# Sliding-window attention regrouped: 32-query groups, shared columns for half-used key blocks, and 128x64 matmul tiles

## The chip, the cores and the metric

The kernel runs on one core of a Trainium2 chip. The metric is the device time of one execution in microseconds (us). Lower is better.

## The reference

Two kinds of layer alternate, twice each, on 2048 tokens of width 512 with 32 heads of 16. The first is linear attention, the second sliding attention in which a query sees itself and the 255 keys before it.

```python
def _A_ref(x, wqkv, wo):            # H = 32, Dh = 16
    q, k, v = ...                   # x @ wqkv, split into heads
    phi = lambda t: jnp.where(t > 0, t + 1, jnp.exp(t)) + 1e-6
    pq, pk = phi(q), phi(k)
    kv = jnp.einsum("bhsd,bhse->bhde", pk, v)
    z = jnp.einsum("bhsd->bhd", pk)
    num = jnp.einsum("bhqd,bhde->bhqe", pq, kv)
    den = jnp.einsum("bhqd,bhd->bhq", pq, z)[..., None] + 1e-6
    return ... (num / den) ... @ wo

def _B_ref(x, wqkv, wo):            # W = 256
    scores = jnp.einsum("bhqd,bhkd->bhqk", q, k) * (Dh ** -0.5)
    mask = (idx[:, None] - idx[None, :] >= 0) & (idx[:, None] - idx[None, :] < W)
    p = _softmax(jnp.where(mask[None, None], scores, -1e9), axis=-1)
    return ... jnp.einsum("bhqk,bhkd->bhqd", p, v) ... @ wo

x = A_x
x = x + _A_ref(_layernorm(x), A_wqkv, A_wo)
x = x + _B_ref(_layernorm(x), B_wqkv, B_wo)
x = x + _A_ref(_layernorm(x), A_wqkv, A_wo)
x = x + _B_ref(_layernorm(x), B_wqkv, B_wo)
```

## The kernel before

The tokens lie in 16 tiles of 128 rows (`xres`), and every stage is written per tile. Each stage is a list of operations, each of which names its engine, what it reads and writes, and a function that emits its instructions. The order of all operations is a table of numbers, `ORDER`; a number with `:a.b` also names the buffers it takes, and one with `'` takes its second engine. The kernel walks the table, takes buffers from rings, and puts a semaphore wait where a dependency needs it. So layers overlap freely: keys of the next linear layer are made while the sliding layer before it still runs.

PE is the matmul engine, ACT does exponentials and copies out of PSUM, DVE the other elementwise work, POOL the reciprocal roots of the layer norm (`rstd`) and the transfers that lay out value blocks, SP the queue of the transposing transfers. PSUM has eight banks, `ps`; one unit of scores takes two pairs of them.

**Linear layer.** `a_kv` normalizes a tile, makes keys (`pk`) and values (`vA`, 17 columns a head with a one for the sum). `kv_mm` multiplies them into sums for groups of eight heads: four 128x128 matmuls of 136 columns a tile. In the first layer these add up in one PSUM pair; in the second, groups of tiles are added by DVE into `kvacc`. `sums` masks off the blocks between different heads, `a_q` and `a_out` do the queries.

**Sliding layer.** `b_qkv` makes queries `qT`, keys `kbd` and values `vbd`. Heads come in pairs: a block of 64 keys of both heads fills the 128 columns of one weight tile, so that scores come out with 2 x 64 keys on the partitions and queries along the columns. `vbd` is the matching block layout of the values, written by four small transfers a tile on POOL. `b_attn` takes 128 queries. They see six 64-key blocks: four middle ones go with all 128 queries, of the oldest only the first 64 queries are needed and of the newest only the last 64. The eight head-pair columns are f (four) x r (four row tiles of 32 that run side by side in PE).

- `sH`: scores of the two half-used blocks, 32 matmuls of 64 columns. `eH0`, `eH1`: two exponentials of 1024 elements into `pH`. `mH0`, `mH1`: two masks of `pH` on DVE, with the triangles of `tri`.
- `s0` to `s3`: scores of the four middle blocks, one unit per f, 16 matmuls of 128 columns. `e00` to `e31`: two exponentials of 1024 elements per unit into `pF`. `m0` to `m3`: one mask of 512 elements per unit.
- `u0h`, `u1h`: products of `pH` with values, 16 matmuls of 34 columns each. A part of 64 queries is padded with zeros to 128 columns, which is what `pH`'s third of zeros is for. `u00` to `u11`: products of `pF`, 16 each.
- `dr`, `dm`: division on DVE. `wo`: output projection and residual.

Tiles 0 and 1 see fewer blocks; the very last tile is written by `b_end`, which masks with matmuls (L1072) instead of DVE.

In the profile: L1016 is `sH`, L1065 `s0` to `s3`, L1044 `eH`, L1086 `e..`, L1052 `mH`, L1104 `m..`, L1122 the products of `pH`, L1134 those of `pF`, L863 and L875 the projections, L921 `kv_mm`, L947 the products of the linear layer's queries, L850 copies out of PSUM, L884 and L887 the two exponential or relu steps of `phi`, L990 the value transfers, L822 `rstd`, L1328 the adds into `kvacc`.

Of the kernel before, what the change touches and what calls it, by code (L numbers as in the profile page):

```python
# [9 lines left out]
ALU = mybir.AluOpType  # L10
# [333 lines left out]
617:4.3 618 619:0 448:2 405 851:0.2.0 415 852 853 416 631 592 632 417:3 625:7.2.5 406 633:0 626 878:4.0.1 622:6.3 623 648 879 880 649 467:3.10.3 468 627' 854  # L344
620 624' 634:4 428:4.0 429 873 469 418:3 650 593 449:2 471 882:0.6.2 883 884 450 482:3.11.1 483 855:1 860:0 861 856 430 431 470 857 621 432:1 451 484 903
651:1 858:1 935:4.6.0 486 862 863:2 859:0 864 885 419:2 420 421 635:3.4 936 874:0.4.3 485 872 433:0 652:0 636 937 607:2.0.0 875 876 608 909:0.6.4 637':1 904
910 911 865:1 62 609' 640:3.0 641 666 653:2.5 638 913:0.4.5 628 654 914 915 643:7.1.1 644 877 886:6 639 667 881 642' 668 629 610 611 655':2 669:2 912 891:3
887 970:0.4.1 645 646 888 702 703 889:3 890:2 938 866:2 892 893 971 972 67 656 894:0 895 657 905:0.6.0 906 867 434:5 435 868 907 944:0.3.3 436 658:2.1 1391
945 908 946 458:6.1 659 459 684 460 472 661:5.2.2 662 670:1 461 660 685 1392 462:3 686 704 917:0.3.1 1393 663' 921:2 922 923 463:2 896:3 918 919 948:0.6.2
924:2 647 916 920 671:5.0 949 950 672 473:3.3 925:1 474 705:3 926:2 1394:0 1395:0 927 487 475 687:1 673:0 1005:0.6.2 1006 476 477:0 928 676:5.2 677 929:0 930  # L350
1007 940:0.3.0 941 464:2 465 897:7 951 942 678' 979:0.5.4 980 688:3 706:2 478:1 931:0 1008 939 466 898 674 1401:4.1 1402 899 981 943 947 952:0.2.5 953
# [4 lines left out]
712:3.0 715:2.2.0 716 1021 1420:1 738 1421:2 1001:1 739 713 1013 709':2 1430 710 1431 717' 1026:5 501 499 500 714' 1022:0.6.1 1023 1024 1409:4.5.2 1410  # L356
1396:2.7.3 1397 1411 1027 711 1025 1412 1053:0.6.2 1413 1422:3.2.1 1423 1432 1052 1398 1054 1055 1028 1424 1399 1400 1031:4 1032 1033 1029:2 1433:3 724:4
1030:1 1434:5 1425 1034:3 1110:0.6.2 1111 1112 725:2.3 726 1426 1035 1427:5.0 727':0 1045:0.3.0 1428 1046 758 718 1002:2 740 741:2 1078 742:0 1003 1047 1429'
1084:0.6.3 1004 1445 1446 683 1056 1414:5.5 730:4.1 1085 1044 1415 1057:0.2.5 1086 1058 728 1048 731 1416' 1440:7.2 1441 732 1059 759:1 1447 729 1435:6.0.2
1442' 1060 1436 1437 1088:0.4.1 1438 1439 1089 1087 502 1061:3 1062 1066:2 1090 1063 1036:0 1064:0 1079 1065:2 1145:0.6.0 1146 760:3 1067 748:5.2 1091 719  # L360
1068 701 1080:0.3.0 1069:1 1070 1147 1081 1082 749 503:6.2 1448:0 504 750' 733:2.1.5 734 743:5.4 735 505 506 1083 736 507:3 1119:0.3.4 1120 1121 744 745':1
1114 751:2.2.1 752 746 508:2 1071:3 747 753' 1149 1092:0.6.2 1093 1037:5 1038 1096:4 1097 1094 1095 1449:3 1039 1123:0.2.5 1124 1098 1125 1101:7 1102 1099:3
# [76 lines left out]
class _Kernel:  # L439
# [496 lines left out]
    def bmask(self, hf):  # L936
        return self.bm8.h[:].unsqueeze(1).unsqueeze(3).to_broadcast([P, 2, 8, 17])
# [443 lines left out]
```

## Time and profile before

| | us |
|---|---|
| median of 3 runs | 414.5 (414.13 to 414.88) |
| profiled execution | 414.87 |
| its span, first to last instruction | 413.6 |
| PE busy | 399.4 |
| ACT busy | 376.6 |
| DVE busy | 370.5 |
| POOL busy | 104.8 |

The granted clock of PE is 1.0 throughout. An engine's busy time counts an instruction from its start to its end; those of PE, and in part those of ACT and DVE, overlap with the next one, so that the time from start to start is the price of one in a row of them. The first layer's part runs from 0 to about 60 us, the linear layer in the middle from about 220 to 260; sliding attention fills the rest, mixed with the neighbouring linear layers.

### The profile page before, as it was taken

How to read it: one execution, taken by the hardware profiler on the slowest of the kernel's cores; microseconds unless marked ns; L12 is line 12 of the kernel's file. 1: busy time of each engine (PE TensorE's matmuls, PEld its weight loads, DVE VectorE, ACT ScalarE, POOL GpSimd, SP SyncE). 2: the span in 40 equal slices, each digit the busy share in tenths (PEclk: the TensorE clock that was granted, in tenths of full speed). 3: DMA queues.
4: the chain of work that ended last, by engine and by line, in shares of the span. 5: the costliest groups of instructions: out<-in, count | busy, mean ns of one | idle time of the engine just before them, and what ended most of it. 6: DMA issues, size and time to landing. Idle time of an engine off the chain costs nothing.

```text
span 413.6 us, 18932 instructions
## 1 busy us (share of the span) xinstructions
PE 399.4 (97%) x8394; PEld 284.3 (69%) x8394; DVE 370.5 (90%) x979; ACT 376.6 (91%) x485; POOL 104.8 (25%) x204
## 2 busy tenths in 40 slices
PE   7999999999999999999999999999999999999998
PEld 2654877776676767777686678676767776867765
DVE  6996799999999999999998999999999999887873
ACT  5998769999999999999999467899999999999996
POOL 2420025162053121411313000260533232311300
DMA  8539224526243235222122102331375453261433
GB/s 259 145 84 217 43 61 80 101 60 99 46 55 57 48 51 69 50 35 61 42 49 55 41 2 40 70 75 32 80 81 76 68 107 34 55 93 30 58 54 92
DMA packets 76808, 29.48 MB, mean 71 GB/s; under 512 B 66352, under 2 KB 74672, under 8 KB 76720
## 3 DMA queue, kind: packets, MB, share of 16 engines
q1 hardware_dynamic: 71424, 22.63, 29.7%
q0 software_dynamic: 4096, 4.46, 6.1%
q8 instruction: 68, 1.11, 1.2%
q10 hardware_dynamic: 1200, 1.11, 0.9%
q14 instruction: 20, 0.16, 0.2%
HBM read 6.29 MB, written 2.10 MB: 20 GB/s over the span
## 4 chain that ended last, share of the span: by engine, by line
PE 50%; ACT 34%; DVE 11%; DMA 3%; issue 1%; SPq 0%; DVEq 0%
ACT pF L1086 24%; PE ps L863 21%; PE ps L875 10%; ACT pH L1044 7%; PE ps L1134 6%; PE ps L1065 5%; PE ps L1122 3%; DVE o L959 2%; DMA w_Av<-in_A_wqkv_dram 2%; PE ps L1016 1%; DVE stats L819 1%; DMA oT<-o 1%; PE ps L921 1%; PE ps L947 1%; DVE pk L890 1%
## 5 line engine op out<-in xcount | busy, mean ns | idle before, releaser
L1086 ACT ACTIVATE pF<-ps 128x1024 bf16<-128x1024 f32 x240 | 229.6, 1083 | 4.4 <-PE ps L1065 2.6
L822 POOL TENSOR_TENSOR rstd<-mv,const 128x1 f32<-128x1 f32 x64 | 37.6, 594 | 211.9 <-DVE mv L820 194.2
L990 POOL DMA_DIRECT2D vbd<-vt x128 | 67.3, 533 | 73.8 <-DVE vt L850 48.6
L1134 PE MATMUL ps<-vbd,pF 128*128 128x34 bf16 x1856 | 62.2, 178 | 1.9 <-issue 1.9
L1044 ACT ACTIVATE pH<-ps 128x1024 bf16<-128x1024 f32 (+1 forms) x64 | 60.3, 1014 | 2.6 <-PE ps L1016 2.3
L1134 PEld LDWEIGHTS ps<-vbd,pF 128*128 128x128 bf16 x1856 | 54.7, 96 | 8.4 <-issue 2.1
L1104 DVE TENSOR_TENSOR pF<-pF,const 128x512 bf16<-128x512 bf16 (+2 forms) x116 | 47.1, 413 | 5.6 <-ACT pF L1086 5.2
L1065 PE MATMUL ps<-qT,kbd 32*128 32x128 bf16 x1920 | 48.7, 217 | 1.9 <-ACT pF L1086 0.6
L884 ACT ACTIVATE E<-ps 128x512 bf16<-128x512 f32 x64 | 38.6, 622 | 10.4 <-PE ps L875 7.8
L819 DVE BATCH_NORM_STATS2 stats<-xres 128x6 f32<-128x512 bf16 x64 | 43.4, 684 | 1.9 <-DMA xres<-in_A_x_dram 1.6
L1052 DVE TENSOR_TENSOR pH<-pH,const 128x1024 bf16<-128x1024 bf16 (+1 forms) x64 | 41.1, 644 | 0.4 <-ACT pH L1044 0.4
L1065 PEld LDWEIGHTS ps<-qT,kbd 32*128 32x128 bf16 x1920 | 28.2, 92 | 17.7 <-ACT pF L1086 7.0
L875 PE MATMUL ps<-xT,w_Bk 128*128 128x128 bf16 x512 | 35.5, 219 | 0.7 <-ACT xT L850 0.3
L875 PE MATMUL ps<-xT,w_Bq 128*128 128x128 bf16 x512 | 35.6, 219 | 0.2 <-ACT pF L1086 0.2
L1122 PEld LDWEIGHTS ps<-vbd,pH 128*128 128x128 bf16 x928 | 29.2, 96 | 9.4 <-issue 3.1
L863 PE MATMUL ps<-w_Av,xTa 128*128 128x512 bf16 (+2 forms) x134 | 33.9, 369 | 1.4 <-DMA w_Av<-in_A_wqkv_dram 1.2
L875 PE MATMUL ps<-xTa,w_Aq 128*128 128x128 bf16 x512 | 34.8, 219 | 0.2 <-DVE pq L888 0.2
L863 PE MATMUL ps<-w_Bv,xT 128*128 128x512 bf16 (+2 forms) x144 | 34.2, 356 | 0.6 <-ACT pF L1086 0.3
L863 PE MATMUL ps<-w_Bo,oT 128*128 128x512 bf16 (+2 forms) x141 | 34.5, 354 | 0.3
L1122 PE MATMUL ps<-vbd,pH 128*128 128x34 bf16 x928 | 32.8, 178 | 1.3 <-DVE pF L1104 0.5
L863 PE MATMUL ps<-w_Ao,oT 128*128 128x512 bf16 (+2 forms) x145 | 33.7, 354 | 0.2
L863 PE MATMUL ps<-w_Ak,xTa 128*128 128x512 bf16 (+1 forms) x131 | 32.7, 374 | 0.6 <-ACT xTa L850 0.5
(98 smaller groups left out, 611.1 us busy)
## 6 DMA issues: line engine op xcount, KB each, us to landing
vbd<-vt POOLq DMA_DIRECT2D x128, 34.0 KB, 2.3
xres<-in_A_x_dram SPq DMA_DIRECT2D x16, 128.0 KB, 5.7
out_dram<-xres SPq DMA_DIRECT2D x15, 128.0 KB, 2.3
oT<-o SPq DMA_TRANSPOSE x60, 2.6
w_Ak<-in_A_wqkv_dram ACTq DMA_DIRECT2D x1, 512.0 KB, 5.5
w_Av<-in_A_wqkv_dram ACTq DMA_DIRECT2D x1, 512.0 KB, 7.6
w_Aq<-in_A_wqkv_dram SPq DMA_DIRECT2D x1, 512.0 KB, 6.6
w_Ao<-in_A_wo_dram SPq DMA_DIRECT2D x1, 512.0 KB, 5.8
```

Source lines behind the costliest of these rows:

```text
L819: s.op(n + ".st", {"DVE": 0.595}, lambda e, en: e.bn_stats(st0, x.h[:]), reads=[x], writes=[st])
L863: i = e.matmul(g.h[:, a:b], xT.h[:, kt, :], w.h[:, kt, a:b], start=(kt == 0), stop=(kt == 3), skip_group_check=True)
L875: i = e.matmul(g.h[:, f * P:(f + 1) * P], w.h[:, kt, f * P:(f + 1) * P], xT.h[:, kt, :], start=(f == 0 and kt == 0), stop=(kt == 3), skip_ ...
L884: s.op(n + ".e", {"ACT": _act_cost(512)}, lambda e, en: e.activation(E.h[:], g.h, ACT.Exp, bias=0.0), reads=[g], writes=[E])
L990: return [e.dma_start(vbd.h[64 * a:64 * a + 64, j, a], vt.h[64 * j:64 * j + 64, a]) for j in range(2)]
L1044: return e.activation(d, c, ACT.Exp, bias=0.0, scale=DH ** -0.5)
L1052: return e.tensor_tensor(v, v, tr, ALU.mult)
L1065: i = e.matmul(ss[r // 2].h[:, r % 2, k * P:k * P + P], kbds[fj[m] // 2].h[32 * r:32 * r + 32, f, fj[m] % 2, :], qT.h[32 * r:32 * r + 32, ...
L1086: s.op("e%d%d" % (u, g), {"ACT": _act_cost(1024)}, lambda e, en, S=ss[g], pb=pb, g=g: e.activation(pb.h[:, 2 * g:2 * g + 2, :], S.h, ACT.E ...
L1104: return e.tensor_tensor(v, v, tr, ALU.mult)
L1122: i = e.matmul(U.h[:, c:c + 34], pH.h[:, 4 * r + f, 64 * a:64 * a + P], vbds[j // 2].h[:, j % 2, :, 4 * f + r, :], start=first[0], stop=Tr ...
L1134: i = e.matmul(U.h[:, c:c + 34], pFs[at[f, m][0]].h[:, r, at[f, m][1] * P:at[f, m][1] * P + P], vbds[fj[m] // 2].h[:, fj[m] % 2, :, 4 * f ...
```

## The change

A tile of 128 queries is seen as four groups of 32. A group needs nine blocks of 32 keys, and the blocks of 64 that are half needed (by one group of the four) are treated apart:

- Keys and values are laid out anew: the 128 columns of a weight tile are now 32 keys of head one, 32 of head two, then the next 32 of each. `kbd` is written in runs of 32, `vbd` by eight transfers of 32 rows a tile instead of four of 64 (`VMOVE`, `vd`).
- `sH` now makes only the scores of 32-key half blocks: 64 matmuls of a 32x64 tile, two half blocks in the two halves of a PSUM column. `eH0`, `eH1` are exponentials of 512 elements into a new ring `Es`.
- `s0` to `s3` score six segments each (`UNIT`): 128, 128, 96, 96, 32 and 32 columns, 512 in all as before. `m..` masks 512 elements in runs of 32. A new DVE operation `x0` to `x3` multiplies `Es` with 0/1 masks (`tri`, now four of 32) into the gaps that `pF`, now 640 wide and a ring of seven, has for it.
- The value products of the two outer blocks (`u0h`, `u1h`) use 64 of `pF`'s columns as a 128x64 weight tile, one for each half of the PSUM partitions; they come after the whole blocks.
- `pH` with its zero fill, its two masks, and `HMD` and `LATE` go. Tiles 0 and 1 move to a function of their own, `b_first`, in the old form with one half-used block.
- `kv_mm` multiplies groups of four heads, as 128x64 tiles of 68 columns, eight a tile instead of four, into one bank instead of two; the first layer does so for four tiles at a time (`KV1`). `kvacc` halves, and its add is one instruction instead of two. `sums` repeats the result for both halves.
- `ORDER` is another table throughout. Counted in the built order: of 127 copies out of PSUM for `vA`, `qT`, `kt` and `vt`, DVE has 59 instead of 80 and ACT 68 instead of 47 (8 of `vA`, 6 of `qT`, 7 of `kt` change over). PE's matmuls go from 8394 to 10327, and places where PE changes between shapes of its tiles from 306 to 381. One input tile fewer is transposed on PE (`BYPE`).

The core of the diff:

```diff
-HMD = ("2.a.", "3.a.")
-BYPE = {("x1.", t) for t in range(4)} | ...
-VMOVE = {"POOL": 1.03}
+BYPE = {("x1.", t) for t in range(3)} | ...
+VMOVE = {"POOL": 2.06}
+KV1 = [4, 4, 4, 4]
...
+UNIT = ((0, 32, 96, 0), (-4, 0, 32, 96), (-2, 0, 128, 128), (1, 96, 32, 256), (-3, 0, 96, 288), (-1, 0, 128, 384))
+FULL = ((0, 0), (-2, 192), (-3, 384), (-1, 512))
+SIDE = ((-4, 128), (1, 320))
...
-            self.r_pF = self.ring("pF", 6, [P, 4, 512])
+            self.r_pF = self.ring("pF", 7, [P, 4, 640])
+            self.r_Es = self.ring("Es", 3, [P, 4, 4, 2, 32])
...
-            self.r_pH = self.preset("pH", 3, [P, 16, 192], self.fill_pH())
...
     def kv_mm(...):
                 for f in range(4):
-                    i = e.matmul(d[f // 2][:, (f % 2) * 136:(f % 2) * 136 + 136], pk.h[:, f * P:(f + 1) * P],
-                                 vA.h[:, 8 * f:8 * f + 8, :], ...)
+                    for c in range(2):
+                        i = e.matmul(g.h[64 * c:64 * c + 64, f * 68:f * 68 + 68], pk.h[:, f * P + 64 * c:f * P + 64 * c + 64],
+                                     vA.h[:, 8 * f + 4 * c:8 * f + 4 * c + 4, :], ..., tile_position=(0, 64 * c))
...
-                o = kbd.h[:, :, :, a * 64:a * 64 + 64].rearrange("p f j c -> p (f j) c")
+                o = kbd.h[:].rearrange("p f j (h a c) -> p (f j h) a c", h=2, a=2)[:, :, a, :]
...
-                return [e.dma_start(vbd.h[64 * a:64 * a + 64, j, a], vt.h[64 * j:64 * j + 64, a]) for j in range(2)]
+                return [e.dma_start(vbd.h[64 * h + 32 * a:64 * h + 32 * a + 32, j, a], vt.h[64 * j + 32 * h:64 * j + 32 * h + 32, a])
+                        for j in range(2) for h in range(2)]
...
+    def b_scores(self, t, qT, kbds, split):
+        Es = self.r_Es.buf()
+        def mmS(e, ss):
+            for f in range(4):
+                for i4, j in enumerate((0, -4, 1, -3)):
+                    h = i4 % 2
+                    for r in range(4):
+                        c = f * 64 + (i4 // 2) * 32
+                        i = e.matmul(ss[r // 2].h[64 * h:64 * h + 64, r % 2, c:c + 32], kbds[t + j // 2].h[32 * r:32 * r + 32, f, j % 2, 64 * h:64 * h + 64],
+                                     qT.h[32 * r:32 * r + 32, f, 32 * i4:32 * i4 + 32], ..., tile_position=(32 * r, 64 * h))
+        ...
+            s.op("eH%d" % g, {"ACT": ...}, ... e.activation(
+                Es.h[:, :, 2 * g:2 * g + 2].rearrange("p f r a c -> p r f (a c)"), S.h[:, :, 0:256]..., ACT.Exp, ...)
+        for f in range(4):
+            def mmF(e, ss, f=f, rs=range(4)):
+                for j, q, n, c in UNIT:
+                    for r in rs:
+                        i = e.matmul(ss[r // 2].h[:, r % 2, c:c + n], kbds[t + j // 2].h[32 * r:32 * r + 32, f, j % 2, :],
+                                     qT.h[32 * r:32 * r + 32, f, q:q + n], ..., tile_position=(32 * r, 0))
+        ...
+                s.op("e%d%d" % (f, g), {"ACT": ...}, ... e.activation(
+                    pb.h[:, 2 * g:2 * g + 2, :].rearrange("p r (n c) -> p r n c", c=160)[:, :, :, 32:160], S.h..., ACT.Exp, ...)
+        ...
+            def put(e, en, pb=pb, f=f):
+                ...
+                x = Es.h[:, f].rearrange("p r a c -> p (r a) c").unsqueeze(2).to_broadcast([P, 8, 2, 32])
+                k = self.tri.h[:, 0:4:3, :].unsqueeze(1).to_broadcast([P, 8, 2, 32])
+                return e.tensor_tensor(v, x, k, ALU.mult)
...
+                        for a, j, p in pFs.side(f, r):
+                            i = e.matmul(U.h[64 * a:64 * a + 64, ((f % 2) * 4 + r) * 34:][:, 0:34], p, vbds[t + j // 2].h[:, j % 2, :, 4 * f + r, :],
+                                         start=False, ..., tile_position=(0, 64 * a))
...
-        groups = [4, 4, 4, 2, 1, 1]
+        groups = KV2                      # the same numbers
```

The order of ACT over three of the last tiles of the second sliding layer, before (`pH` and `pF` are exponentials, `qT` a copy):

```order
L850 ACTIVATE qT<-ps 128x512
L1086 ACTIVATE pF<-ps 128x1024 x2
L1044 ACTIVATE pH<-ps 128x8x2x64 x2
L1086 ACTIVATE pF<-ps 128x1024 x6
L1044 ACTIVATE pH<-ps 128x8x2x64 x2
L1086 ACTIVATE pF<-ps 128x1024 x10
```

And now, at the same place:

```order
L862 ACTIVATE qT<-ps 128x512
L1101 ACTIVATE pF<-ps 128x8x128 x6
L1068 ACTIVATE Es<-ps 128x2x4x64 x2
L862 ACTIVATE vt<-ps 128x32x16
L1101 ACTIVATE pF<-ps 128x8x128 x10
L1068 ACTIVATE Es<-ps 128x2x4x64 x2
```

The pair on `pH`, 1024 elements each, has become a pair on `Es` of 512; the exponentials of `pF` keep their count and size.

The order of PE near the end of the first sliding layer, before (`pH` and `pF` against `vbd` are value products, `qT` against `kbd` scores):

```order
L1016 MATMUL ps<-qT,kbd 128x64 x32
L863 MATMUL ps<-w_Bv,xT 128x512 x2
L863 MATMUL ps<-w_Av,xTa 128x512 x4
L863 MATMUL ps<-w_Ak,xTa 128x512 x4
L1122 MATMUL ps<-vbd,pH 128x34 x16
L1065 MATMUL ps<-qT,kbd 128x128 x16
L1134 MATMUL ps<-vbd,pF 128x34 x32
```

And now:

```order
L1061 MATMUL ps<-qT,kbd 64x32 x64
L875 MATMUL ps<-w_Av,xTa 128x512 x3
L875 MATMUL ps<-w_Av,xTa 128x448
L875 MATMUL ps<-w_Av,xTa 128x64
L1078 MATMUL ps<-qT,kbd 128x96 x4
L1078 MATMUL ps<-qT,kbd 128x32 x4
L1078 MATMUL ps<-qT,kbd 128x128 x4
L1078 MATMUL ps<-qT,kbd 128x32 x4
L1078 MATMUL ps<-qT,kbd 128x96 x4
L1078 MATMUL ps<-qT,kbd 128x128 x4
L1016 MATMUL ps<-vbd,pF 128x34 x32
L1028 MATMUL ps<-vbd,pF 64x34 x16
```

A unit of scores has become six segments, the half-block products (L1028) stand behind the whole ones of the same heads, and they have a tile shape of their own, as have the scores for `Es` (L1061).

More of the change, by code (lines that the diff above doesn't have):

```diff
@@ L345 @@
[L345 to L348, printed above, removed]
@@ L439, with full, use, both @@
+FULL = ((0, 0), (-2, 192), (-3, 384), (-1, 512))
+SIDE = ((-4, 128), (1, 320))
+class _Parts(list):
+    def full(self, f, r):
+        return [(j, self[f].h[:, r, c:c + P]) for j, c in FULL]
+    def use(self, f):
+        return [self[f]]
+    def both(self, g):
+        return self[2 * g:2 * g + 2]
+    def side(self, f, r):
+        return [(a, j, self[f].h[:, r, c:c + 64]) for a, (j, c) in enumerate(SIDE)]
 class _Kernel:
@@ L989, in vd @@
             def vd(e, en, a=a):
-                return [e.dma_start(vbd.h[64 * a:64 * a + 64, j, a], vt.h[64 * j:64 * j + 64, a]) for j in range(2)]
-            s.op("vd%d" % a, VMOVE, vd, reads=[vt], part=[vbd], dma=True, tail=0.3).dmas = 2
+                return [e.dma_start(vbd.h[64 * h + 32 * a:64 * h + 32 * a + 32, j, a], vt.h[64 * j + 32 * h:64 * j + 32 * h + 32, a]) for j in range(2) for h in range(2)]
+            s.op("vd%d" % a, VMOVE, vd, reads=[vt], part=[vbd], dma=True, tail=0.3).dmas = 4
         return qT, kbd, vbd
@@ L997, in b_attn @@
         o = self.r_o.buf()
-        m0 = {0: 3, 1: 1}.get(t, 0)
         split = last and t == self.T - 1
-        fj = [2 * t - 3 + m for m in range(4)]
-        pcs = [(a, j) for a, j in ((0, 2 * t - 4), (1, 2 * t + 1)) if j >= 0]
-        pH = self.r_pH.buf()
-        pFs = []
-        def scores(n, pb, js, mm, cost):
-            ss = [self.pG.buf(2), self.pG.buf(2)]
-            kbs = [qT, self.key, self.far] + [kbds[j // 2] for j in js]
-            s.op(n, {"PE": cost}, lambda e, en: mm(e, ss), reads=kbs, writes=ss, new=ss + [pb], mode="r", kind="score")
-            return ss
@@ L1048, in b_attn @@
-        for g in range(2) if s.at[0] in HMD else ():
-            def mkH(e, en, g=g):
-                v = vH(g)
-                tr = self.tri.h[:].unsqueeze(1).to_broadcast([P, 8, 2, 64]) if len(pcs) == 2 else self.tri.h[:, 1:2, :].to_broadcast([P, 8, 64])
-                return e.tensor_tensor(v, v, tr, ALU.mult)
-            s.op("mH%d" % g, {"DVE": 0.065 + 0.00054 * 512 * len(pcs)}, mkH, reads=[self.tri, mH[g]], part=[pH])
-        nm = 4 - m0
-        at = {(f, m): divmod(f * nm + m - m0, 4) for f in range(4) for m in range(m0, 4)}
@@ L1108, in b_attn, with pvF, pvH @@
+        pFs = self.b_first(t, qT, kbds) if t < 2 else self.b_scores(t, qT, kbds, split)
         if split:
-            return self.b_end(t, o, pH, pFs, pcs, fj, vbds, w)
-        def use(f):
-            return [pFs[u] for u in sorted({at[f, m][0] for m in range(m0, 4)})]
+            return self.b_end(t, o, pFs, vbds, w)
         for g in range(2):
             U = self.pG.buf()
-            first = [True]
-            def pvH(e, en, g=g, U=U, first=first):
+            for f in (2 * g, 2 * g + 1):
+                def pvF(e, en, f=f, g=g, U=U):
+                    for r in range(4):
+                        for m, (j, p) in enumerate(pFs.full(f, r)):
+                            i = e.matmul(U.h[:, ((f % 2) * 4 + r) * 34:][:, 0:34], p, vbds[t + j // 2].h[:, j % 2, :, 4 * f + r, :],
+                                         start=(f == 2 * g and r == 0 and m == 0), stop=True, skip_group_check=True)
+                    return i
+                js = [j for j, _ in ((0, 0), (-2, 0), (-3, 0), (-1, 0)) if 2 * t + j >= 0]
+                s.op("u%d%d" % (g, f % 2), {"PE": 0.0252 * 4 * len(js)}, pvF, reads=pFs.use(f) + [vbds[j] for j in sorted({t + j // 2 for j in js})], writes=[U],
+                     new=[U] if f == 2 * g else [], kind="sum")
+            def pvH(e, en, g=g, U=U):
@@ L1306, in graph @@
         s.at = ("1.", base)
-        self.sums(lambda hf: kvS.h[:, hf, 0:272], kvz)
+        self.sums(lambda: kvS.h[:, 0:272], kvz)
         b1 = base + 0.1
```

458 lines of the change are left out of this document (227 added, 231 removed), and 95 rows, old and new, of the table ORDER.

## The prediction

> **What bounds the kernel now.** I read the page first, then the time by stage, the waits, the chain of waits and, for prices, the groups kept apart by shape and pieces of the timeline. The page:
>
> ```profile
> span 413.6 us, 18932 instructions
> PE 399.4 (97%) x8394; PEld 284.3 (69%) x8394; DVE 370.5 (90%) x979; ACT 376.6 (91%) x485; POOL 104.8 (25%) x204
> PE 50%; ACT 34%; DVE 11%; DMA 3%; issue 1%; SPq 0%; DVEq 0%
> ```
>
> Three engines are nearly full, so the average does not say which one sets the end. The busy time by stage does (columns PE, PEld, DVE, ACT, POOL, each with its instruction count):
>
> ```profile
> 0.00:60.00 60.00, 56.53 (x499) 34.55 (x500) 49.45 (x159) 46.57 (x81) 11.51 (x31) 1.00 0.52 135
> 60.00:220.00 160.00, 156.77 (x3580) 113.64 (x3578) 150.08 (x384) 154.57 (x188) 46.00 (x85) 1.00 0.36 61
> 220.00:260.00 40.00, 39.41 (x613) 29.28 (x610) 37.28 (x104) 28.35 (x48) 5.49 (x10) 1.00 0.16 30
> 260.00:400.00 140.00, 135.80 (x3407) 98.68 (x3409) 127.35 (x316) 137.80 (x158) 41.83 (x78) 1.00 0.41 64
> ```
>
> In the two stretches with sliding attention (60 to 220, 260 to 400, 300 us together) ACT is busy 292.4 us and idle 7.6; DVE has 22.6 us free. In the other stretches ACT has room and PE is the full one. The busy time of PE counts the pipelined ends of matmuls, so its 97% hides waits. The waits show on which side they lie:
>
> ```profile
> DVE dn L1144 <- PE ps L1134: 9.8, 20, 1.1
> PEld ps L1065 <- ACT pF L1086: 7.0, 27, 0.4
> ACT pF L1086 <- PE ps L1065: 2.6, 8, 0.7
> ```
>
> PE's score matmuls (L1065) wait 27 times for an exponential (L1086) to give back its PSUM banks; the reverse happens 8 times. And where the chain of waits passes the late tiles of the second sliding layer, it is exponentials end to end:
>
> ```profile
> 341.94 1.83 ACT pH L1044 x2
> 343.78 9.17 ACT pF L1086 x10
> 352.94 1.83 ACT pH L1044 x2
> ```
>
> So ACT's work is what the attention stretches last, with PE close behind.
>
> **ACT, part by part.** Before, a tile of 128 queries takes ten exponentials of 1024 elements: two for pH, eight for pF. After, the two become two of 512 (Es), in 28 of 32 tile passes (tiles 0 and 1 of each layer keep their form). The chain above gives 9.17 / 10 = 0.917 us for one of 1024. One of 512 is read from two that follow each other:
>
> ```profile
> 153.37 0.63 ACT L884 ACTIVATE E<-ps 128x512 bf16<-128x512 f32 x1
> 153.85 0.64 ACT L887 ACTIVATE pq<-ps 128x512 bf16<-128x512 f32 x1
> ```
>
> That is 0.48 us from start to start, and 56 x (0.917 - 0.48) = 24.5 us less. Against this, the order gives ACT 21 copies out of PSUM that DVE did before (8 vA, 6 qT, 7 kt): 21 x 0.48 = 10.1 us more, 6.2 of it (qT, kt) in the attention stretches. ACT there: 292.4 - 24.5 + 6.2 = 274.1, or 18.3 us less.
>
> **DVE.** The two masks of pH go; four of 512 elements on pF stay, cut into runs of 32 instead of 64; four products that put Es into pF come.
>
> ```profile
> L1104 DVE TENSOR_TENSOR pF<-pF,const 128x512 bf16<-128x512 bf16 x110 | 44.7, 414 | 5.4 <-ACT pF L1086 4.9
> L888 DVE TENSOR_TENSOR pq<-pq,E 128x512 bf16<-128x512 bf16 x32 | 13.1, 412 | 0.4
> 152.08 0.71 DVE L1104 TENSOR_TENSOR pF<-pF,const 128x512 bf16<-128x512 bf16 x2
> 158.93 0.69 DVE L1052 TENSOR_TENSOR pH<-pH,const 128x1024 bf16<-128x1024 bf16 x1
> 159.53 0.25 DVE L1144 RECIPROCAL dn<-ps 128x16 f32<-128x16 f32 x1
> 154.57 0.67 DVE L850 CAST vA<-ps 128x512 bf16<-128x512 f32 x1
> 155.16 0.28 DVE L885 TENSOR_SCALAR E<-E 128x512 bf16<-128x512 bf16 x1
> L1328 DVE TENSOR_TENSOR kvacc<-ps,kvacc 128x272 f32<-128x272 f32 x10 | 3.9, 433 | 0.0
> ```
>
> Two 512 masks take 0.71, so the second adds 0.71 - 0.414 = 0.30. A pH mask takes 159.53 - 158.93 = 0.60, a copy 155.16 - 154.57 = 0.59. Added: 112 x 0.30 = 33.6. Gone: 56 x 0.60 = 33.6, 21 x 0.59 = 12.4 in copies, and six of twelve adds of the key-value sums, 6 x 0.43 = 2.6. Net -15 us (-7.7 in the attention stretches). The runs of 32 are in no row. The lower end is 0: runs of 64 (414 ns) cost what one contiguous run does (412). The upper end is that such a product runs like the copy with fp32 input, 0.59 instead of 0.30 on 220 instructions, +64 us. I take 0, the nearer row.
>
> **PE.** These rows price it; busy time less the mean duration is the time from the first start to the last.
>
> ```profile
> L1134 PE MATMUL ps<-vbd,pF 128*128 128x34 bf16 x1856 | 62.2, 178 | 1.9 <-issue 1.9
> L1065 PE MATMUL ps<-qT,kbd 32*128 32x128 bf16 x1920 | 48.7, 217 | 1.9 <-ACT pF L1086 0.6 <-DVE dn L956 0.2
> L1016 PE MATMUL ps<-qT,kbd 32*128 32x64 bf16 x960 | 12.7, 189 | 1.1 <-ACT pF L1086 0.2
> L1072 PE MATMUL ps<-const 32*128 32x32 bf16 x64 | 1.3, 172 | 0.0
> L947 PE MATMUL ps<-kvz,pq 128*128 128x136 bf16 x128 | 13.3, 223 | 0.4 <-DVE o L959 0.4
> L875 PE MATMUL ps<-xT,w_Bq 128*128 128x128 bf16 x512 | 35.6, 219 | 0.2 <-ACT pF L1086 0.2
> L863 PE MATMUL ps<-w_Bo,oT 128*128 128x512 bf16 x107 | 30.8, 380 | 0.3
> 156.14 0.56 PE L1134 MATMUL ps<-vbd,pF 128*128 128x34 bf16 x16
> 156.63 0.40 PE L1065 MATMUL ps<-qT,kbd 32*128 32x128 bf16 x16
> 156.96 0.62 PE L875 MATMUL ps<-xT,w_Bq 128*128 128x128 bf16 x8
> 158.84 0.41 PE L1016 MATMUL ps<-qT,kbd 32*128 32x64 bf16 x32
> 161.41 0.41 PE L947 MATMUL ps<-kvz,pq 128*128 128x136 bf16 x4
> 161.74 1.02 PE L863 MATMUL ps<-w_Bo,oT 128*128 128x512 bf16 x4
> 400.20 0.26 PE L1072 MATMUL ps<-const 32*128 32x32 bf16 x16
> ```
>
> - Value products on half blocks (960): now (0.56 - 0.178) / 15 = 25.5 ns each. After, two 128x64 tiles may run side by side: 12.7 ns at best, 25.5 if nothing overlaps. Four row tiles side by side took (0.41 - 0.189) / 7 = 32 ns per four of 64 columns, that is 25% over a quarter of four single 25.5s (8 against 6.4); with the same loss a pair gives 16 ns: 960 x (16 - 25.5) = -9.1 us (-12.3 to 0).
> - Key-value products of the linear layers (32 tiles): four of 136 columns at (0.41 - 0.223) / 3 = 62 ns, 0.25 us. After, eight of half the width in pairs, by the same loss 0.15: -3.2 us (-4 to 0).
> - Scores of a whole unit (112): four quads of 128 columns become two of 128, two of 96, two of 32. A quad of 128 takes (0.40 - 0.217) / 3 = 61 ns, of 64 32 ns, of 32 (0.26 - 0.172) / 3 = 29 ns, of 96 between, 46. So 272 instead of 244 ns: +3.1 us.
> - Scores for Es (28): 64 matmuls of 32x64, in eights at 32 ns 0.26, as before; in fours 16 x 29 = 0.46. 0 to +5.7; I take 0, since row tiles already overlap fully.
> - Changes of tile shape: in the order they rise from 306 to 381. L1134's last start is 156.14 + 0.56 - 0.178 = 156.52 and L1065 starts 0.11 later, 0.085 over its usual 25.5 ns; L1065's last start is 156.81 and L875 follows 0.15 later, 0.09 over a quad. 75 x 0.09 = +6.7 us.
>
> Sum: -9.1 - 3.2 + 3.1 + 0 + 6.7 = -2.5 us (-6.5 to +15.5). PE gains almost nothing: what the pairs save, the changes of shape take back.
>
> [...] No row of this trace has a column tile.
>
> **POOL and the rest.** The value blocks are laid out by eight small transfers a tile instead of four.
>
> ```profile
> L990 POOL DMA_DIRECT2D vbd<-vt x128: 516/523/677, 61.2 to 390.6; - x128
> DVE xn L825 <- POOL rstd L822: 1.9, 4, 0.8
> ```
>
> At 0.52 us each, 128 more keep POOL 67 us longer: 172 of 400, no bound. But whatever stands behind them on its queue, the reciprocal roots (L822) for the layer norm, can come 2.1 us later, and the blocks too. DVE waits for L822 only 4 times now, 1.9 us; nobody waits for L990. I cost it at 0 behind that lead, +5 if the lead is short.
>
> **Sum.** In the attention stretches ACT loses 18.3 us. Next late is PE. Its rows give what it needs: 2880 value products x 25.5 ns = 73.4; 1536 of L875 at (0.62 - 0.219) / 7 = 57 ns = 88; 636 of 512 columns (split ones counted once) at (1.02 - 0.380) / 3 = 213 ns = 135.5; 480 and 240 quads = 37; 256 of 136 columns = 16; 306 changes of shape x 0.09 = 27.5; together 377 of 413.6. So some 36 us are start, end and waits, about 24 of them in these 300 us. Taking 18.3 there would leave PE 6 us of waits in 300, so I take three quarters of it, 14 us, and nothing in the other stretches. 414.87 for the profiled execution becomes 400.9; the median of the runs shown, 414.5, lies 0.4 below it, so **400.5 us**. From PE's side the same number reads 377 - 2.5 + 26 us of start, end and waits.
>
> **Rivals.**
> 1. *More.* The room on all three engines (ACT -14, DVE -15) is used in the linear stretches too, and all of the 18.3 comes through: 414.5 - 18.3 - 4 = 392. For: DVE waits for PE 20 times, which a fuller order may close. Against: PE is full there. Chance 0.12.
> 2. *The half-block pairs gain nothing.* Their weights are loaded no faster than in the 128x128 form, and each product still takes 25.5 ns: PE +6.6, so 377 + 6.6 + 26 = 409 to 410. For: no row shows a column tile, and ACT waits for PE in 8 places already. Against: row tiles side by side lose only 25%. Chance 0.14. [...]
> 3. *Slower.* No column tile overlaps another: PE +15.5, and 377 + 15.5 + 26 = 418.5. With the key-value products and the Es scores at their dear ends (+6.4 so far), it decides from about 22 ns per half-block product on. For: Es issues 64 small matmuls in a block that had 32. Chance 0.12.
> 4. *The change doesn't do what it says:* the Es exponential, read and written in 64-element pieces, costs as much as one of 1024 elements. Then ACT only has the 10.1 us of copies more: 414 to 422. The old one-sided form, also in pieces of 64, speaks against it, at 0.6 us:
>
> ```profile
> L1044 ACT ACTIVATE pH<-ps 128x512 bf16<-128x512 f32 x8 | 4.7, 600 | 0.8 <-PE ps L1016 0.7
> ```
>
> Chance 0.04.
>
> The forecast has 0.58 (396 to 406). The range 391 to 412 leaves out rivals 3 and 4 and part of 1, about 0.2. A measurement of this kernel can tell about 0.2% (0.8 us) from no change. Faster: 0.58 + 0.12 + 0.14 less an edge of 0.01 for rival 2 = 0.83; same 0.02 (that edge, and one of rival 4); slower 0.15.
>
> **What would show it.** ACT's 512-element Es group x56 near 620 ns mean and ACT busy near 361; the put products x112 near 414 ns; half-block products starting 13 to 18 ns apart, Es scores in about 0.42 us a block; PE's wait for L1086's successor shrinking, PE with the longest share of the chain. Wrong would be: put products near 600 ns, half-block starts 25 ns or more apart, POOL's lead gone (DVE waiting for rstd by more than 5 us), or PE waits unchanged although ACT has 20 us of idle time in the attention stretches.

## The result and the profile after

| kernel | median, us | runs | ratio to before, 95% interval |
|---|---|---|---|
| before | 414.53 (414.13 to 414.88) | 4 | |
| after | 437.92 (435.0 to 438.76) | 4 | 1.0552 [1.0500, 1.0604] |

The change makes the kernel 23.4 us slower; the forecast was 400.5 with a range of 391 to 412. The profiled execution took 437.3 us. Its page:

```profile
span 436.0 us, 22960 instructions
PE 411.8 (94%) x10327; PEld 296.1 (68%) x10327; DVE 364.1 (84%) x1011; ACT 365.0 (84%) x503; POOL 166.5 (38%) x332
PEclk9999999999999999899999999989989999999996
q8 instruction: 84, 1.38, 1.4%
PE 68%; ACT 18%; DVE 8%; issue 4%; DMA 2%; DVEq 0%
```

ACT has most of the relief that was forecast (365.0 busy, from 376.6, 11.6 us less where 24.5 - 10.1 = 14.4 were forecast), and PE's part of the chain has grown from 50% to 68%. The clock, full throughout before, now has slices below 9. Queue q8 carries instructions (68 packets of 16 KB before, 84 now); they are taken to be PE's, whose instructions go from 17,040 to 20,896 with them, 251 and 249 a packet. The busy time by stage:

```profile
60.00:220.00 160.00, 154.28 (x4319) 113.60 (x4317) 139.97 (x382) 144.87 (x194) 73.38 (x143) 0.99 0.36 59
260.00:400.00 140.00, 130.25 (x3739) 97.40 (x3737) 117.46 (x313) 119.44 (x151) 63.18 (x126) 0.98 0.35 60
```

In the attention stretches ACT was idle 7.6 of 300 us before; now it is idle 35.7, and PE is idle 15.5, from 7.4; nobody has taken up ACT's relief. These are the same clock times in both kernels, while the changed kernel's stages come up to 20 us later; taken about where its attention lies (60 to 230 and 272 to 420), ACT is idle 36.1 us of 318 and PE 16.5, the same picture. The waits tell on which side they lie (us, times, longest; those of ACT and DVE first, then PE's own):

```profile
ACT pF L1101 <- PE ps L1078: 19.2, 33, 1.7
DVE dn L1038 <- PE ps L1028: 18.9, 23, 2.0
ACT Es L1068 <- PE ps L1061: 13.0, 18, 2.5
DVE xn L837 <- POOL rstd L834: 3.3, 6, 0.7
PE ps L1078 <- issue: 4.2, 6, 1.3
PE ps L1016 <- issue: 3.5, 5, 1.4
PE ps L1028 <- issue: 2.7, 4, 1.2
PE ps L1061 <- issue: 2.1, 4, 1.5
```

ACT and DVE wait for PE, and PE waits for "issue": for nothing that the profile shows another engine do. Before there was one such row, 3 times and 1.9 us:

```profile
PE ps L1134 <- issue: 1.9, 3, 0.8
```

With one more at L1083 (1.0 us) it is now 20 times and 13.5 us. The timeline shows one of them (start, duration; the idle time before a row in brackets), and below it the clock around it:

```profile
173.01 0.68 PE L1061 MATMUL ps<-qT,kbd 32*64 32x32 bf16 x64
173.62 0.57 PE L1016 MATMUL ps<-vbd,pF 128*128 128x34 bf16 x16
174.12 0.43 PE L1028 MATMUL ps<-vbd,pF 128*64 128x34 bf16 x16
174.48 0.30 PE L1078 MATMUL ps<-qT,kbd 32*128 32x96 bf16 x12
176.12 0.40 PE L1078 MATMUL ps<-qT,kbd 32*128 32x32 bf16 x12 [1.33 <-issue]
176.45 1.89 PE L875 MATMUL ps<-w_Av,xTa 128*128 128x512 bf16 x4
```

```profile
172.00:174.50 2.50, 2.50 (x119) 2.05 (x119) 2.13 (x5) 1.96 (x4) 0.04 (x1) 1.00 0.03 7
174.50:176.20 1.70, 0.37 (x25) 0.24 (x24) 1.00 (x3) 0.35 (x1) 1.70 (x4) 0.87 0.00 0
176.20:178.50 2.30, 2.30 (x17) 0.81 (x17) 0.43 (x1) 1.93 (x2) 2.30 (x6) 0.50 1.47 145
```

In the middle of a unit of 24 matmuls, which wait for no other engine between them, PE stands still for 1.33 us; afterwards, from 176.2 to 178.5, the granted clock is 0.50, and four matmuls of 512 columns take 1.89 us instead of 1.03. The transfers from 173.4 to 176.2, in 40 slices, are one packet of q8:

```profile
DMA  0900000000000000000000000000000000000000
DMA packets 1, 0.02 MB, mean 6 GB/s; under 512 B 0, under 2 KB 0, under 8 KB 0
q8 instruction: 1, 0.02, 2.9%
```

It starts at 173.52, lands at 174.81, and PE goes on 1.31 us later. At the other stops the time from landing to going on is 1.2 to 1.6 us. Counted in the trace, the stops lie a multiple of 126 to 128 matmuls apart, and so many matmuls with their loads are 252 to 256 instructions. The 20,896 PE instructions (a load and a matmul 10327 times, and 242 others, nearly all semaphores) over 84 packets are 249 each, close to that. So each stop is put at a border between two 16 KB pieces of some 250 instructions, an estimate from these counts.

### The profile page after: what moved, and what is told of

The parts are those of the page before. It is cut to its first block, busy times and chain, and to the rows that moved or that the text cites. A ratio compares the mean times of both kernels' runs of the same rounds, so it can differ in the third digit from the quotient of the medians.

```text
span 436.0 us, 22960 instructions
## 1 busy us (share of the span) xinstructions
PE 411.8 (94%) x10327; PEld 296.1 (68%) x10327; DVE 364.1 (84%) x1011; ACT 365.0 (84%) x503; POOL 166.5 (38%) x332
## 4 chain that ended last, share of the span: by engine, by line
PE 68%; ACT 18%; DVE 8%; issue 4%; DMA 2%; DVEq 0%
PE ps L875 24%; PE ps L887 15%; ACT pF L1101 10%; PE ps L1016 9%; PE ps L1078 8%; PE ps L1061 4%; PE ps L1028 4%; ACT pF L1178 2%; DVE o L967 2%; ACT E L896 2%; DMA w_Av<-in_A_wqkv_dram 2%; DVE dn L966 1%; ACT pq L899 1%; ACT vA L862 1%; PE ps L955 1%
## 5 line engine op out<-in xcount | busy, mean ns | idle before, releaser
L1101 ACT ACTIVATE pF<-ps 128x1024 bf16<-128x1024 f32 x224 | 214.0, 1038 | 23.0 <-PE ps L1078 19.2
L998 POOL DMA_DIRECT2D vbd<-vt x256 | 127.9, 507 | 41.6 <-DVE vt L862 22.9
L1078 PE MATMUL ps<-qT,kbd 32*128 32x96 bf16 (+2 forms) x2688 | 50.2, 198 | 5.8 <-issue 4.2
L1119 DVE TENSOR_TENSOR pF<-Es,const 128x512 bf16<-128x512 bf16 x112 | 44.8, 413 | 4.7 <-PE ps L1083 2.7
L1110 DVE TENSOR_TENSOR pF<-pF,const 128x512 bf16<-128x512 bf16 x108 | 43.7, 414 | 4.1 <-ACT pF L1101 3.7
L1078 PEld LDWEIGHTS ps<-qT,kbd 32*128 32x128 bf16 x2688 | 31.6, 92 | 21.5 <-issue 8.9
L1068 ACT ACTIVATE Es<-ps 128x512 bf16<-128x512 f32 x56 | 30.5, 600 | 13.4 <-PE ps L1061 13.0
L875 PE MATMUL ps<-w_Ak,xTa 128*128 128x512 bf16 (+2 forms) x133 | 34.8, 376 | 0.6 <-DMA w_Ak<-in_A_wqkv_dram 0.5
L887 PEld LDWEIGHTS ps<-xT,w_Bq 128*128 128x128 bf16 x512 | 31.2, 100 | 4.2 <-issue 0.9
L887 PEld LDWEIGHTS ps<-xTa,w_Aq 128*128 128x128 bf16 x512 | 30.4, 98 | 5.3 <-DVE pq L900 0.4
```

Of the source, the lines that this page charges most:

```text
L875: i = e.matmul(g.h[:, a:b], xT.h[:, kt, :], w.h[:, kt, a:b], start=(kt == 0), stop=(kt == 3), skip_group_check=True)
L887: i = e.matmul(g.h[:, f * P:(f + 1) * P], w.h[:, kt, f * P:(f + 1) * P], xT.h[:, kt, :], start=(f == 0 and kt == 0), stop=(kt == 3), skip_ ...
L998: return [e.dma_start(vbd.h[64 * h + 32 * a:64 * h + 32 * a + 32, j, a], vt.h[64 * j + 32 * h:64 * j + 32 * h + 32, a]) for j in range(2) ...
L1068: s.op("eH%d" % g, {"ACT": _act_cost(512)}, lambda e, en, g=g, S=ss[g]: e.activation(Es.h[:, :, 2 * g:2 * g + 2].rearrange("p f r a c -> p ...
L1078: i = e.matmul(ss[r // 2].h[:, r % 2, c:c + n], kbds[t + j // 2].h[32 * r:32 * r + 32, f, j % 2, :], qT.h[32 * r:32 * r + 32, f, q:q + n], ...
L1101: s.op("e%d%d" % (f, g), {"ACT": _act_cost(1024)}, lambda e, en, S=ss[g], pb=pb, g=g: e.activation(pb.h[:, 2 * g:2 * g + 2, :].rearrange(" ...
```

## The experiments

Three theories. **S (supply):** PE uses up a piece of some 250 instructions before the next is there; 10327 short matmuls do that where 8394 did not. **W (work):** the new matmul shapes are dearer than costed. **The forecast's premise:** ACT's relief comes through if nothing else gets in its way. Beside them, the transfers on POOL and the half-block products. "Waits" counts PE's waits for issue as above (20 and 13.5 us in the changed kernel, 3 and 1.9 in the one before), without those of up to 0.5 us among 512-column matmuls, since 80 to 89 matmul records are missing from each of the traces of e1_split to e4_es16. (The changed kernel's trace is complete; there this leaves out two real stops, 0.7 us.) Each ratio is to the kernel before on the same chip.

| run | PE matmuls | median, us | before, us | ratio, 95% interval | waits |
|---|---|---|---|---|---|
| e1_split | 10314 | 429.06 | 414.81 | 1.0313 [1.0242, 1.0385] | 14, 9.3 us |
| e2_halfexp | 8394 | 414.25 | 414.81 | 0.9977 [0.9955, 1.0000] | 3, 2.5 us |
| e3_u16 | 9431 | 425.69 | 414.81 | 1.0260 [1.0227, 1.0293] | 12, 5.9 us |
| e4_es16 | 8983 | 414.73 | 414.81 | 0.9982 [0.9948, 1.0015] | 5, 4.3 us |
| e5_u16_es16 | 8087 | 408.44 | 414.20 | 0.9881 [0.9841, 0.9922] | 2, 0.7 us |
| e6_vd4 | 10327 | 435.21 | 414.20 | 1.0467 [1.0412, 1.0523] | 19, 12.6 us |
| e7_side128 | 10327 | 436.48 | 414.20 | 1.0537 [1.0519, 1.0554] | 16, 11.5 us |
| e8_phase | 10391 | 443.06 | 414.20 | 1.0657 [1.0589, 1.0726] | 19, 12.7 us |
| e9_halfpv | 7962 | 411.24 | 414.93 | 0.9923 [0.9884, 0.9962] | 1, 0.2 us |
| e10_halfboth | 7962 | 409.10 | 414.93 | 0.9864 [0.9820, 0.9908] | 3, 2.5 us |
| e11_bphase | 8434 | 414.51 | 414.93 | 0.9990 [0.9972, 1.0008] | 3, 0.9 us |

**e1_split: more instructions, the same work, in the kernel before.**

```diff
-  e.matmul(ss..[k * P:k * P + P], kbds.., qT.h[.., f, :], start=(k == 0), ...)
+  e.matmul(ss..[k * P:k * P + 64], kbds.., qT.h[.., f, 0:64], start=(k == 0), ...)      # for r in 4 rows
+  e.matmul(ss..[k * P + 64:k * P + P], kbds.., qT.h[.., f, 64:128], start=False, ...)   # for r in 4 rows
```

> The kernel before, with each 128-column score matmul of a whole unit (L1065) issued as two of 64 columns: 1920 more PE instructions (10314 instead of 8394), nothing else changed. Theory S (supply): PE's instructions arrive in pieces of fixed size, and a denser stream of short matmuls uses a piece up before the next one is there; then many waits of 0.3 to 1.6 us appear inside blocks of equal matmuls (3 now, 21 in the changed kernel), with a lower granted clock after them, and the time rises to 424 to 436. Theory W (work): the changed kernel is slower because its new matmul shapes are dearer; here two quads of 64 columns cost 2 x 32 = 64 ns against 61, 480 x 3 ns = 1.4 us, so 415 to 417 and no new waits inside blocks.

It takes 13 to 14 us more (10 to 16 by the interval), as S says. An undisturbed unit (first and last rows of its eight, and what follows) goes from 152.82 to 153.17, 0.35 us; before it was 156.63 to 156.96, 0.33: over 120 units at most 2.4 us. The rest are stops like this one:

```profile
152.82 0.21 PE L1065 MATMUL ps<-qT,kbd 32*128 32x64 bf16 x4
...
153.04 0.20 PE L1069 MATMUL ps<-qT,kbd 32*128 32x64 bf16 x4
153.17 0.62 PE L875 MATMUL ps<-xT,w_Bk 128*128 128x128 bf16 x8
```

```profile
385.09 0.19 PE L1069 MATMUL ps<-qT,kbd 32*128 32x64 bf16 x2
386.71 0.20 PE L1069 MATMUL ps<-qT,kbd 32*128 32x64 bf16 x2 [1.44 <-issue]
```

So 1920 more PE matmuls cost this kernel 11 to 14 us, with ACT, DVE and every tile shape as they were.

**e8_phase: the same stream, shifted by 64 matmuls.**

```diff
+                    c = 384 if n == 2 else D if i < 3 else 32
-        s.op("warm", {"PE": 4.5}, warm(11), reads=[wm], writes=[wg], new=[wg])
+        s.op("warm", {"PE": 4.5}, warm(75), reads=[wm], writes=[wg], new=[wg])
```

> The changed kernel with 75 warm-up matmuls at the very start (3 of 512 columns and 72 of 32) instead of 11, in the same 5 us before the data is there: every later PE instruction stands 64 matmuls later in the stream. S: the pieces' borders fall 64 matmuls away from where they fell, so that none of the blocks that waited without a semaphore waits at its old place, and as many others do; numbered from the changed kernel's own count, the waits lie 64 (mod 128) from the old ones. Time about the same, 428 to 442, as chance puts the borders on denser or thinner places. Rival (the waits belong to the code at that place, a bank, a transfer or a buffer): the same blocks wait at the same places, time 437 to 439.

All 20 stops of the changed kernel are gone from their matmuls: there each starts 3 to 49 ns after the one before. New stops are at other blocks, and numbered from the start of the stream they lie on the same steps of 126 to 128 (three on the same number in both: 8263, 9662 and 10042). The block of Es scores that stopped for 1.46 us in the changed kernel, and the same block here:

```profile
312.50 0.61 PE L1061 MATMUL ps<-qT,kbd 32*64 32x32 bf16 x56
314.57 0.22 PE L1061 MATMUL ps<-qT,kbd 32*64 32x32 bf16 x8 [1.46 <-issue]
```

```profile
320.61 0.79 PE L1061 MATMUL ps<-qT,kbd 32*64 32x32 bf16 x64
```

The stops belong to the place in the stream, not to the code, a bank or a buffer. The 5 us more, 1 us over the upper end expected, come from the edit itself: with the longer warm-up the first fetch in the trace begins at 8.62 us instead of 2.18, and PE's first transposes come at 11.15 instead of 5.49 us, 1.5 us after it has landed. The same matmuls are 5.7 us late at 65 us and 5.6 at 389 us (up to 12.9 in between, where the stops lie otherwise).

**e3_u16 and e4_es16: fewer instructions in the changed kernel.**

```diff
-UNIT = ((0, 32, 96, 0), (-4, 0, 32, 96), (-2, 0, 128, 128), (1, 96, 32, 256), (-3, 0, 96, 288), (-1, 0, 128, 384))
+UNIT = ((0, 0, 128, 0), (-2, 0, 128, 128), (-3, 0, 128, 256), (-1, 0, 128, 384))       # e3_u16
...
+                for r in range(4):                                                      # e4_es16
+                    i = e.matmul(ss[r // 2].h[:, r % 2, f * 64:f * 64 + 64], kbds[t].h[32 * r:32 * r + 32, f, 0, :],
+                                 qT.h[32 * r:32 * r + 32, f, 0:64], ..., tile_position=(32 * r, 0))
```

> The changed kernel, with each whole unit of scores in four segments of 128 columns (16 matmuls) instead of six (24): 896 fewer PE instructions (9431 instead of 10327); the segments no longer belong to the right queries. W: the unit's work falls from 272 to 244 ns, 112 x 28 ns = 3.1 us, so 434 to 436. S: the waits inside blocks (22, 13.9 us, and the clock after them) fall by about half as the stream gets thinner: 425 to 430.

> The changed kernel, with the scores for Es as 16 matmuls of a 32x128 tile and 64 columns instead of 64 of a 32x64 tile and 32 columns: 1344 fewer PE instructions (8983 instead of 10327) and one tile shape fewer; the scores are not those of the right keys. W: a block falls from 0.61 to about 0.13 + 0.06 us, 28 x 0.45 = 12.6 us, so 424 to 426. S in addition: most waits inside blocks go too, 412 to 419.

Both land where S and W together put them, 12.2 and 23.2 us below the changed kernel, against 3.1 and 12.6 by the work alone as it was expected. The waits fall from 20 to 12 and 5.

**e5_u16_es16: both.**

> The changed kernel with both edits: units in four segments and Es scores in 16 matmuls of a 32x128 tile, 8087 PE instructions, fewer than the kernel before has (8394); the scores are not those of the right queries and keys. If the two act apart from each other, 437.9 - 12.2 - 23.2 = 402.5. W alone: 437.9 - 3.1 - 13.4 = 421. S with W: the waits inside blocks are about gone after the first edit already, so the second has less left to take: 404 to 410.

408.4 lies between 402.5 and 421: with 8087 matmuls the stops are gone (2, 0.7 us) and the clock is 1.0, so the second edit finds less to take. This is the change without its extra matmuls, ACT's relief, half-block pairs and new order included, and it is 5.8 us faster than before (3.2 to 6.6 by the interval of the ratio), not 14.

**e6_vd4 and e7_side128: POOL and the half-block pairs.**

```diff
-  return [e.dma_start(vbd.h[...], vt.h[...]) for j in range(2) for h in range(2)]
+  return [e.dma_start(vbd.h[...], vt.h[...]) for j in range(2) for h in range(1)]        # e6_vd4
...
-  i = e.matmul(U.h[64 * a:64 * a + 64, ...][:, 0:34], p, ..., tile_position=(0, 64 * a))
+  i = e.matmul(U.h[:, ...][:, 0:34], p, ...)                                             # e7_side128, p of 128 columns
```

> The changed kernel with four value transfers a tile on POOL instead of eight; half of the value rows of a tile are left out. If the transfers or what stands behind them on POOL cost time: 2 to 5 us less, 433 to 436. If they lie beside other work, as DVE's 3.3 us of waits for rstd says: 437 to 439, no difference beyond what single runs scatter.

> The changed kernel with the 896 half-block value products as 128x128 tiles over all PSUM partitions instead of pairs of 128x64 ones; same count of instructions, and the column-tile shape gone from these blocks; the products are not the right ones. By the rows: 25.5 instead of about 18 ns inside a block, 896 x 7 = +6.3 us, and some 75 to 110 changes of shape fewer at 0.07 to 0.09, -5 to -10. So W: 432 to 439. S: the products stretch the stream by 0.1 us a block, so a few waits inside blocks fewer, 1 to 3 us: 430 to 437.

Four transfers fewer a tile gave 1.0467 against the changed kernel's 1.0552, 3.5 us, but the intervals overlap: 0 to some 7 us, not settled. The stops stay (19, 12.6 us), so the added transfers do not make them. The half blocks in 128x128 form take 25.5 ns each inside a block instead of the pairs' 16.2, some 8 us more in all, and the kernel's time is the same. What goes against it is some 55 changes of shape fewer (at 0.09 us 5 us) and 2.0 us less of stops; how much each is worth was not taken apart.

**e2_halfexp, e9_halfpv, e10_halfboth: what bounds the kernel before.** Work is taken from ACT alone, from PE alone, and from both.

```diff
-                    d = d.rearrange("p (r f) a c -> p r f a c", r=2)
+                    c, d = c[:, :, :, 0, :], d[:, :, 0, :].rearrange("p (r f) c -> p r f c", r=2)   # e2, e10
...
-                        for a, j in pcs:
+                        for a, j in pcs[-1:]:                                                     # e9, e10
```

> The kernel before, with the two exponentials of pH in 28 tile passes taken over 512 elements instead of 1024; the other half of pH stays zero, so half of the outer scores are left out. It is ACT's relief alone: 56 x (0.917 - 0.48) = 24.5 us of ACT's time, 20 to 24 of it in the attention stretches, with PE's and DVE's work untouched. The forecast's premise (ACT sets the pace, PE has some room): three quarters of it comes through, 414.5 - 15 to 18 = 397 to 400. Rival (PE binds together with ACT): the relief is worth little, 408 to 413, with PE's waits for pF gone and ACT idle instead.

> The kernel before, with one of the two half-used blocks left out of the value products in 28 tile passes: 448 of 128x34 fewer, 448 x 25.5 ns = 11.4 us less of PE's work, nothing taken from ACT or DVE. The forecast's premise (ACT's exponentials are what the attention stretches last): hardly anything, 412 to 414. PE holds the end alone: 403 to 405. Both together: in between, 406 to 411.

> The kernel before, with both edits: exponentials of pH over 512 elements (ACT -24.5 us; alone it gave 0.6) and half of pH's value products left out (PE -11.4 us). PE holds the end alone: the same as with the products alone, within 1 us. PE and ACT hold it in turn: the two together give more than the sum of the single ones, by 3 to 8 us, 395 to 403.

ACT's 24.5 us gave 1.0 us (0.0 to 1.9), PE's 11.4 gave 3.2 (1.6 to 4.8), both together 5.6 (3.8 to 7.5). ACT's 24.5 us are by the price from start to start; its busy time on the page falls by 17.4, from 376.6 to 359.2, and 2.6 us of the difference are a longer zero fill of pH that the edit needs. Neither "ACT sets the pace" nor "PE alone holds the end" survives; both together give 1.4 us more than the two alone, which lies inside the intervals. The chains, of e2_halfexp, of e9_halfpv and of e10_halfboth:

```profile
PE 56%; DVE 23%; ACT 15%; issue 3%; DMA 3%; SPq 0%; DVEq 0%
```

```profile
ACT 51%; PE 23%; DVE 20%; DMA 4%; issue 2%; POOL 0%; SPq 0%; DVEq 0%; POOLq 0%
```

```profile
PE 38%; DVE 29%; ACT 28%; issue 2%; DMA 2%; POOL 1%; DVEq 0%
```

Relieve ACT, and the chain goes over PE and DVE; relieve PE, and it goes over ACT; relieve both, and the three share it. In e2_halfexp the group on pH is busy 36.0 us (60.3 before), and ACT then waits 17.9 us for the score matmuls, where before it was 2.6:

```profile
L1044 ACT ACTIVATE pH<-ps 128x512 bf16<-128x512 f32 x64 | 36.0, 626 | 2.4 <-PE ps L1016 2.0
...
ACT pF L1086 <- PE ps L1065: 17.9, 33, 2.5
```

**e11_bphase: the kernel before, shifted by 40 matmuls.**

```diff
-        w2 = s.op("warm2", {"PE": 0.6}, warm(2, 384), reads=[wm], writes=[wg])
+        w2 = s.op("warm2", {"PE": 0.6}, warm(42, 16), reads=[wm], writes=[wg])
```

> The kernel before, with the second warm-up as 42 matmuls of 16 columns instead of two of 384, in the same idle time: all later PE instructions stand 40 matmuls later in the stream. S: the three blocks that wait now without a semaphore (near 137, 148 and 402 us) no longer do, others may; 411 to 416, faster by up to 2 us if the borders fall on places where PE is slow anyway. Rival (waits belong to the place in the code): the same three wait, 414 to 415.

The three stops at 137, 148 and 402 us are gone, three others are at 108, 301 and 347 us, and the time is the same. No run pointed to a version that keeps the whole computation and beats the kernel before.

## Why the prediction was wrong

**Prices that held.** These rows of the changed kernel answer to the terms:

```profile
L1068 ACT ACTIVATE Es<-ps 128x512 bf16<-128x512 f32 x56 | 30.5, 600 | 13.4 <-PE ps L1061 13.0
L1119 DVE TENSOR_TENSOR pF<-Es,const 128x512 bf16<-128x512 bf16 x112 | 44.8, 413 | 4.7 <-PE ps L1083 2.7 <-PE ps L1078 1.9
L998 POOL DMA_DIRECT2D vbd<-vt x256 | 127.9, 507 | 41.6 <-DVE vt L862 22.9 <-DVE mv L832 5.9 <-ACT vt L862 5.8
L1028 PE MATMUL ps<-vbd,pF 128*64 128x34 bf16 x928 | 26.3, 187 | 2.8 <-issue 2.7
L1061 PE MATMUL ps<-qT,kbd 32*64 32x32 bf16 x1792 | 19.9, 188 | 2.8 <-issue 2.1
L1028 PEld LDWEIGHTS ps<-vbd,pF 128*64 128x64 bf16 x928 | 20.5, 112 | 6.0 <-issue 3.1
L1016 PEld LDWEIGHTS ps<-vbd,pF 128*128 128x128 bf16 x1856 | 55.9, 96 | 13.0 <-issue 4.3
```

- Exponentials of Es (600 ns) and products in runs of 32 (413 ns) cost what was taken; rival 4 and the +64 us end are out. POOL's lead holds: DVE waits for rstd 3.3 us, from 1.9. DVE's busy time fell by 6.4 us (370.5 to 364.1) where the sum had 15; the sum used times from start to start, so busy time alone does not settle that term.
- Half-block pairs: a block of 16 takes (0.43 - 0.187) / 15 = 16.2 ns each, the forecast's 16. Rival 2 is out as a mechanism, and so is rival 3 for the pairs (it needed about 22 ns); the other reason given for rival 3, the 64 small matmuls of Es, came true, as below. A load of 64 columns shows 112 ns, longer than the 96 ns of a full one (the last two rows), as rival 2 supposed of the loads, but the 25.5 ns per product that it drew from that did not come.
- Units of 24: first to last start 214 ns, from 188, so +26 against +28 forecast. Changes of shape: the trace gives +6.8 us, forecast +6.7.

**The term that was mis-sized: scores for Es.** The block at 173.01 has (0.68 - 0.188) = 0.49 us from first to last start, 7.8 ns per matmul. Forecast was 0.26, "since row tiles already overlap fully"; the two column halves gave nothing on top of that, and a matmul of half the columns cost no less than one of 64 (7.1 ns before); why, no run here shows. 28 blocks come to +7.2 us instead of 0, beyond the upper end of +5.7. With this the PE sum is +4.7 instead of -2.5; the trace has -1.0 inside blocks and +6.8 at changes of shape, +5.8.

**The cost that was not on the list: supply.** The prediction counted 1933 more matmuls and 75 changes of shape, and priced each by its time in a row, with nothing for the rate at which PE's instructions arrive. Adding up the times from start to start over all of PE's matmuls, the two traces differ by 22.2 us, and those +5.8 leave +16.3. That is a net figure. Set against the usual time between the same two shapes, matmuls that started after a wait for issue came 17.9 us late, from 2.3 before (the idle time, and the end of the matmul ahead of each), and matmuls that started at a granted clock of 0.50 came 6.3 us late, from none: +21.9 us together. By the same count waits for other engines shrink by 1.7 us and other late starts by 2.3, and the usual times rise by 4.3 (the 5.8 above, averaged another way). e1_split gives a cost of the same kind (11 to 14 us for 1920 matmuls) without any other part of the change, and e8_phase ties the stops to the place in the stream.

**The step that failed on the gain side: "three quarters of it, 14 us".** It took ACT's idle 7.6 us in 300 to mean that ACT sets the pace, and the 27 waits for an exponential to mean that PE waits for ACT. But that row is of weight loads (PEld), which run beside matmuls (busy 284.3 us, with PE's 399.4, in a span of 413.6); PE's own row in the kernel before is far smaller:

```profile
PE ps L1065 <- ACT pF L1086: 0.6, 3, 0.2
```

e2_halfexp takes the same 24.5 us from ACT, with PE's and DVE's work as it was, and gets 1.0. The 24 us of start, end and waits that the prediction found for PE in these 300 us were read as room; but the chain passes from PE to ACT to DVE and back, and where one is shortened it goes over the others. The forecast's gain was out of reach without any stop: e5_u16_es16, which has the relief, no extra matmuls and less work in its scores, stands at 408.4. That is inside the range 391 to 412, but with less than half of the 14 us; with supply and the dear Es scores taken away, as there, the range holds by luck, since the reason given for it is wrong all the same. The prediction named a sign for this, 20 us of idle ACT with PE's waits unchanged: ACT's idle time came as 35.7 us, and PE's did not fall but rose, from 7.4 to 15.5.

So it went to the slower side, and rival 3 had only the Es scores of it right: PE's time rose by 22 us. Supply and the clock behind it come to that much alone; changes of shape and Es scores, less what the pairs saved, add 4 to 6 us, and shorter waits elsewhere take about 4 off. The relief of ACT had hardly anything to set against it.

What stays open: what a stop would cost without the lower clock after it, since the trace divides the two (15.6 and 6.3 us) but no run has the one without the other; why a fetch does not begin earlier; whether POOL's transfers cost 0 or up to some 7 us; and what the new order alone is worth, as no run has the old work in it.

## What to carry to other kernels

Where three engines are each about 90% busy in a fixed order, take the relief alone (here half of pH's exponentials left out) before counting it as gain: here 24.5 us of ACT were worth 1 us. When a change cuts matmuls into smaller ones, count PE's instructions as well as its nanoseconds; a stream that stopped 3 times with 8394 matmuls in 414 us stopped 20 times with 10327. A wait for "issue" inside a block of equal matmuls is the sign, and moving the stream by a few dozen matmuls at the start shows in one run whether it belongs to the stream or to the code.

## What the runs showed of the hardware

- The packets of q8 hold 16 KB each, one for some 250 PE instructions (17,040 to 68 packets in the kernel before, 20,896 to 84 in the changed one). In the changed kernel a fetch takes 0.9 to 1.7 us, and a stopped PE goes on 1.2 to 1.6 us after it has landed. In the changed kernel's 20 stops the fetch had begun 2.2 to 3.1 us before PE went on, and the 31 to 98 matmuls that PE had left to run by then did not last that long.
- The granted clock fell to 0.50 four times inside the changed kernel's work, from 175.8, 285.0 and 315.7 us for 3.4 us each and from 424.9 us for 6.8 us. Each time a stop of 1.0 to 1.5 us had ended at most 1.2 us before, or was still on. Most stops were not followed by it, one of 1.45 us at 361.0 us among them.
- With four row tiles side by side a matmul took 7.1 ns for 64 columns (the old `sH`) and 7.8 ns for 32 columns in half-width tiles (the new one, in the block at 173.01): halving both the columns and the tile saved nothing.
